# The second product of a mixture layer, computed transposed: w_out stationary and g moving

## Chip, cores and metric

The kernel runs on one core of one Trainium2 chip. The metric is the device time in microseconds (us) of one execution. Before the change the median of 3 runs is 1168.23 us (1168.09 to 1169.08).

## What is computed

The reference, cut to what matters, with 8 batches, 12 heads, 448 tokens of a batch, 64 features of a head, d_model 768 and d_ff 2048:

```python
scores = q @ k.T / sqrt(64) - log(448)          # per batch and head, 448 x 448
attn = 1 / (1 + exp(-scores))
x = (attn @ v), the heads side by side           # 3584 tokens x 768
h = x @ w_in                                     # 3584 x 2048
g = h - tanh(h)
out = g @ w_out                                  # 3584 x 768, f32
```

## The kernel before

The work goes batch by batch. The features of x lie on the partitions, so x of one batch is six tiles of 128 x 448 (features x tokens). TensorE computes with a *stationary* operand, which a weight load (LDWEIGHTS, shown as PEld) puts into the array, and a *moving* operand that streams past it; the stationary operand's columns become the partitions of the result, which lands in a PSUM bank.

To come near f32, most operands are split into a high and a low f16 half, and each product is three matmuls: high x high, high x low, low x high. The steps of one batch:

- **Attention** (`stream`, and for batch 0 `attention32`). Scores `sc` (`scores`, L393), the sigmoid `a` on ScalarE (L404), its split `ahl` on ScalarE and VectorE (L410, L411), the product with v into `acc` (`av`, L424).
- **First product** (`moe1`, `product` L772). For each of 8 pairs of 128-wide blocks of d_ff: w_in is stationary, x is moving (448 columns), result `ph`, two PSUM banks. `mix` (L804) then works off `ph`: two ScalarE activations (`u` L810, `th` L812), VectorE steps (L814, L815, L821, L825), more activations and a select (L828). `halves` (L763) writes the tile of g: its high half on ScalarE (L765), then its low half on VectorE (L766). One such tile `g` holds two blocks f of d_ff, each 128 x 448.
- **Second product** (`moe2`). In the kernel before, a 128-token slice of g is the stationary operand and a half of w_out's rows (384 of 768 columns) is the moving one. For batches 1 to 7 there are three tiles of 128 tokens; in each, the loop over the 16 blocks f runs the three products for both halves, into the banks `po0` and `po1`, and ScalarE (L889) and VectorE (L893) copy one bank each out, scaled, and SP stores it (`store`). Batch 0 takes the halves one after the other, since the second half of w_out is still being converted. The last 64 tokens are the remainder: `por` (L904) is computed with two half-wide matmuls side by side, copied by VectorE (L913) and stored in two pieces.

For batches 1 to 6, the attention of the next batch is put between the matmuls of the second product. `moe2` is a generator; after each of its steps `second` looks at `now` and issues the attention blocks whose position has come (the table `BLOCKS`, in steps of six matmuls: 8, 11, 16 and so on; `BLOCKS1` for batch 1). The rest of the last tile's `mix` and its `halves` are issued at the positions `TAIL`, 1 to 5. Batch 7 has no attention behind it. In batch 0 everything, the conversion and split of the weights too (L186, L201, L237 to L240), is laid out by hand in the string `ORDER`, one letter for a step; `P` is a step of the second product.

Each engine takes its instructions in the order of issue. `po` lies in two PSUM banks that take turns (tag `mm`), and the output tile `o` in two buffers.

Of the kernel before, what the change touches and what calls it, by code (L numbers as in the profile page):

```python
# [10 lines left out]
F32 = mybir.dt.float32  # L11
# [3 lines left out]
AF = mybir.ActivationFunctionType  # L15
ALU = mybir.AluOpType
# [3 lines left out]
P = 128  # L20
D = 64
# [12 lines left out]
class Builder:  # L34
# [5 lines left out]
    ORDER = (  # L40
        "lurmlorumsrrsrrmmlussmvvrrssvvrlrssvvrrvruvlssrurssvvrrssvlrrsvvvursrsvs"
        "vrrssvrsrrvvvvRrRrRRRMrRRRnRrRRGMRRwtMttRtRBtwRRtMwBgttMtRtRttMBttRtRttM"
        "tMBBtRttRMtBttMttMtRxtRtBRAtMtttAMtBttMttAttAttMMtAtPPtaRPRBPtBbtCaBCBAC"
        "PtFCCPBPCPPBZPPPCSBCPPBZCBCPPCCBPCCCSZBPPCCCPCXBaaAPaPPPBAPPaaaBBSPPSPSZ"
        "PSZSPPPPPPPSPBPPPZPPPNPZPSPZPSSNNPPSZPPZSSPPPPPPPPPPPP"
    )

    BLOCKS = (8, 11, 16, 20, 20, 20, 27, 32, 36, 36, 36, 43, 48, 52, 52)
# [242 lines left out]
    def w_out_scale(self, e):  # L291

        V = self.nc.vector
        self.w_out_bound(e)
        m = self.bound[e]
        total = self.sm.tile([P, 1], F32, name="wtot2")
        V.scalar_tensor_tensor(total, m, 1.05, m, op0=ALU.mult, op1=ALU.mult)
        S, inv = self.scale_of(total, f"swo{e}")
        self.Swo.append(S)
        V.tensor_copy(self.iSwo[:, e : e + 1], inv)  # L300
        h = slice(e * D, (e + 1) * D)
        V.tensor_copy(self.iSwo[h, 2:3], inv[h])

    def split_w_out(self, e):
        for f in range(0, self.NF, 2):
# [530 lines left out]
    def moe2(self, b, gs):  # L836
        nc = self.nc
        S = self.S
        ks = self.ks
        iK = self.sm.tile([P, 3], F32, name="iK")  # L840
        n = 1 if b == 0 else 3
        nc.vector.tensor_scalar(iK[:, :n], self.iSwo[:, :n], self.iSg, None, op0=ALU.mult)
        H = self.HALF
        base = b * S
        prods = ((0, 0), (0, 1), (1, 0))
        last = (self.NF - 1, 2)

        def store(o, j0, n, cols, queue=nc.sync):
            queue.dma_start(self.out[base + j0 : base + j0 + n, cols], o)

        nt = S // P

        def products(po, tk, f, e):
            for n, (x, w) in enumerate(prods):
                for i in e:
                    nc.tensor.matmul(  # L856
                        po[i][:, :H],
                        gs[f // 2][:, x, f % 2, tk * P : (tk + 1) * P],
                        self.wo[:, i * self.NF + 2 * ks[f // 2] + f % 2, w],
                        start=(f == 0 and n == 0),  # L860
                        stop=((f, n) == last),
                    )

        if b == 0:
            for e in range(2):
                for tk in range(nt):
                    po = {e: self.ps.tile([P, 512], F32, name="po", tag="mm", bufs=2)}
                    for f in range(0, self.NF, 2):
                        products(po, tk, f, (e,))
                        products(po, tk, f + 1, (e,))  # L870
                        if f + 2 == self.NF:
                            if (e, tk) == (1, 0):
                                nc.vector.tensor_scalar(iK[:, 1:], self.iSwo[:, 1:], self.iSg, None, op0=ALU.mult)
                            o = self.op.tile([P, H], F32, name="oh", tag="o", bufs=2)
                            nc.scalar.activation(o, po[e][:, :H], AF.Copy, scale=iK[:, e : e + 1])
                            store(o, tk * P, P, slice(e * H, (e + 1) * H))
                        yield 980
        else:
            for tk in range(nt):
                if b + 1 == self.B and tk % 2:  # L880
                    both = self.ps.tile([P, 2, 512], F32, name="po", tag="sc", bufs=2)
                    po = [both[:, e] for e in range(2)]
                else:
                    po = [self.ps.tile([P, 512], F32, name=f"po{e}", tag="mm", bufs=2) for e in range(2)]
                for f in range(self.NF):
                    products(po, tk, f, (0, 1))
                    if f == self.NF - 1:
                        o = self.op.tile([P, self.DM], F32, name="o", tag="o", bufs=2)
                        nc.scalar.activation(o[:, :H], po[0][:, :H], AF.Copy, scale=iK[:, 0:1])  # L889
                        if (b, tk) == (1, 0):  # L890
                            nc.scalar.activation(o[:, H:], po[1][:, :H], AF.Copy, scale=iK[:, 1:2])  # L891
                        else:
                            nc.vector.tensor_scalar(o[:, H:], po[1][:, :H], iK[:, 1:2], None, op0=ALU.mult)  # L893
                        store(o, tk * P, P, slice(0, self.DM))
                    yield 980
        nm = nt * P
        if b + 2 < self.B:
            po = self.ps.tile([P, 512], F32, name="por", tag="mm", bufs=2)
        else:
            po = self.ps.tile([P, 2, 512], F32, name="por", tag="sc", bufs=2)[:, 0]  # L900
        for f in range(self.NF):
            for n, (x, w) in enumerate(prods):
                for e in range(2):
                    nc.tensor.matmul(  # L904
                        po[e * D : (e + 1) * D, :H],
                        gs[f // 2][:, x, f % 2, nm:S],
                        self.wo[:, e * self.NF + 2 * ks[f // 2] + f % 2, w],
                        start=(f == 0 and n == 0),
                        stop=((f, n) == last),
                    )  # L910
            yield 560
        o = self.op.tile([P, H], F32, name="orem", tag="o", bufs=2)
        nc.vector.tensor_scalar(o, po[:, :H], iK[:, 2:3], None, op0=ALU.mult)  # L913
        for e in range(2):
            queue = nc.scalar if e and b + 1 == self.B else nc.sync
            store(o[e * D : (e + 1) * D], nm, S - nm, slice(e * H, (e + 1) * H), queue)


    def build(self):
        nc, tc = self.nc, self.tc  # L920

        def const(name, value, n=1):
            t = self.const.tile([P, n], F32, name=name)
            nc.vector.memset(t, value)
            return t

        self.nls = const("nls", -math.log(self.S))
        self.b1 = const("b1", B1)
        self.b2 = const("b2", B2)
        self.b3 = const("b3", -CUT * CUT)  # L930
        self.tiny = const("tiny", TINY)
        self.ih0 = const("ih0", 1.0)
        self.ihk0 = const("ihk0", KAPPA)
        self.iSwo = const("iswo", 1.0, 3)
        self.sums = [const(f"ss{i}", 0.0, 6) for i in range(2)]
        self.Swo = []
        self.sums_out, self.bound = [[], []], [None, None]
        self.xs32, self.x2b = False, []
        pieces = list(self.pieces())
        nA = 4 * self.NC  # L940
        E = mybir.EngineType
        with tc.manual_schedule(engines={E.PE, E.Activation, E.DVE, E.Pool}):
            nB = nA + self.NF + self.EARLY
            self.stage = tc.alloc_tile_pool(name="stage", bufs=2, reuse_waits="tile")
            self.blocks = self.stream()
            self.first(
                self.convert(pieces[:nA], "attention"),
                self.convert(pieces[nA:nB], "mixture"),
                self.convert(pieces[nB:], "product"),
            )  # L950
        with tc.manual_schedule(engines={E.PE, E.Activation, E.DVE, E.Pool, E.SP}):
            for b in range(1, self.B):
                self.batch(b)
        self.gp.release()
# [128 lines left out]
    def second(self, b, blocks, alone, events):  # L1083

        step = lambda: next(self.blocks)
        events += [(p, step) for p in blocks]
        scales = []

        def norms():
            scales.append(self.batch_scales(self.xs, False))  # L1090
            next(scales[0])

        if blocks:
            end = blocks[alone]
            events.append((end + 3, norms))
            events += [(p, lambda: next(scales[0], None)) for p in (end + 5, end + 7)]
        events.sort(key=lambda e: e[0])
        full = self.NF * (self.S // P)
        for k, _ in enumerate(self.moe2(b, self.gs)):
            now = k + 1 if k < full else full + (k + 1 - full) / 2  # L1100
            while events and events[0][0] <= now:
                events.pop(0)[1]()
        assert not events
# [34 lines left out]
```

## Time and profile before

| What | Value |
|---|---|
| median of 3 runs | 1168.23 us |
| lowest and highest run | 1168.09, 1169.08 us |
| span of the profiled execution (its own time, no other is given for it) | 1167.9 us |
| TensorE busy | 1155.8 us (99%) |
| VectorE (DVE) busy | 907.0 us (78%) |
| ScalarE (ACT) busy | 867.1 us (74%) |
| granted TensorE clock, mean | 1.000 |
| matmuls of the second product, full and remainder | 2304 and 768 |

The span runs from the first to the last instruction of one execution; it lies 0.3 us under the median of the runs. Rows of groups give the code line, engine, operation, output <- inputs with their shape and count, then busy time and mean duration (ns), then idle time of the engine before them and what ended it. Rows of the timeline give the start, the duration (both us, counted from the span's start), the engine, the line and the count of instructions merged. Matmuls overlap in such rows: a row's duration holds the latency of its last one, so rates are read from one row's start to the next row's start. Line numbers are those of the kernel before, unless the text says otherwise.

### The profile page before, as it was taken

The page shows a single profiled execution, that of the slowest core. Times are in us where ns is not written, and L with a number is a line of the kernel's source. Part 1 is how long each engine was busy: PE and PEld are TensorE (multiplying, and loading weights), DVE is VectorE, ACT ScalarE, POOL GpSimd, SP SyncE. Part 2 cuts the span into 40 slices and gives each one's busy share as a digit, 9 for nine tenths or more (in the row PEclk, how much of TensorE's full clock was granted, in tenths as well). Part 3 has the DMA queues.
Part 4 walks back from the last instruction along what each step waited for, and adds up shares of the span by engine and source line. Part 5 has one row for each costly group of instructions (what it writes and reads, how often), then busy time and mean ns, then how long its engine had stood idle before and what let it go on. Part 6 is the DMA issues. An engine that isn't in the chain of part 4 may idle for free.

```text
span 1167.9 us, 18941 instructions
## 1 busy us (share of the span) xinstructions
PE 1155.8 (99%) x7585; PEld 601.7 (52%) x7585; DVE 907.0 (78%) x1308; ACT 867.1 (74%) x1195; POOL 77.9 (7%) x58
## 2 busy tenths in 40 slices
PE   9999999999999999999999999999999999999998
PEld 2345434555555555555555555555555555555565
DVE  6999999789777896679867897778976799646930
ACT  7988996588975888768888588867887688745820
POOL 0000000000120002200021000200022000300000
PEclk9999999999999999999999999999999999999999
DMA  9942171000222002210022101210012100000000
GB/s 361 355 160 64 34 226 52 34 7 1 78 72 64 11 1 77 62 53 1 17 75 62 40 1 31 79 58 26 1 55 84 52 1 8 23 27 8 1 15 34
DMA packets 34056, 70.43 MB, mean 60 GB/s; under 512 B 3888, under 2 KB 21040, under 8 KB 33968
## 3 DMA queue, kind: packets, MB, share of 16 engines
q1 hardware_dynamic: 33744, 68.89, 18.2%
q8 instruction: 59, 0.97, 0.4%
q10 hardware_dynamic: 224, 0.33, 0.1%
q14 instruction: 29, 0.24, 0.1%
HBM read 58.20 MB, written 11.01 MB: 59 GB/s over the span
## 4 chain that ended last, share of the span: by engine, by line
PE 73%; ACT 1%; issue 0%; DVE 0%; ACTq 0%
PE ph L772 28%; PE po L856 27%; PE sc L393 6%; PE acc L424 6%; PE por L904 5%; ACT ahl L410 0%; ACT a L404 0%; PE pbn L343 0%; PE nm L689 0%; ACT sqn L335 0%; ACT x L438 0%; ACT Q L368 0%; DVE orem L913 0%; ACT x L453 0%; ACT o L891 0%
## 5 line engine op out<-in xcount | busy, mean ns | idle before, releaser
L856 PE MATMUL po<-wo,g 128*128 128x384 f16 x2304 | 389.2, 326 | 2.8 <-DVE wo L240 1.4
L772 PE MATMUL ph<-xhl,wi 128*128 128x448 f16 x2016 | 382.6, 352 | 0.0
L856 PEld LDWEIGHTS <-g 128*128 128x128 f16 x2304 | 220.6, 98 | 168.6 <-issue 25.3
L772 PEld LDWEIGHTS <-wi 128*128 128x128 f16 x2016 | 196.7, 98 | 185.0 <-issue 2.1
L411 DVE SCALAR_TENSOR_TENSOR ahl<-a,ahl 128x896 f16<-128x896 f32 x126 | 161.6, 1318 | 127.9 <-ACT ahl L410 127.8
L404 ACT ACTIVATE a<-sc,nls,rn 128x896 f32<-128x896 f32 x147 | 155.7, 1090 | 38.6 <-PE sc L393 38.2
L810 ACT ACTIVATE u<-ph,ih 128x896 f32<-128x896 f32 x64 | 64.4, 1006 | 77.0 <-PE ph L772 75.1
L410 ACT ACTIVATE ahl<-a 128x896 f16<-128x896 f32 x126 | 113.2, 941 | 0.6
L393 PE MATMUL sc<-Q,K 64*128 64x448 f16 x1008 | 100.8, 353 | 0.8 <-DVE th L815 0.6
L814 DVE SCALAR_TENSOR_TENSOR m<-ph,ihk,u 128x896 f32<-128x896 f32 x64 | 73.4, 1147 | 27.5 <-ACT th L812 27.2
L765 ACT ACTIVATE g<-m,Sg 128x896 f16<-128x896 f32 x64 | 66.7, 1042 | 35.2 <-DVE m L828 28.2
L828 DVE COPY_PREDICATED m<-u,th 128x896 f32<-128x896 uint32 x64 | 77.3, 1207 | 6.9 <-ACT u L827 0.9
L424 PE MATMUL acc<-ahl,vhl 128*64 128x448 f16 (+1 forms) x864 | 80.6, 356 | 0.1
L766 DVE SCALAR_TENSOR_TENSOR g<-m,Sg,g 128x896 f16<-128x896 f32 x64 | 73.4, 1146 | 6.8 <-ACT g L765 6.7
L455 POOL TENSOR_TENSOR x<-x 128x448 f32<-128x448 f32 x24 | 27.1, 1129 | 765.5 <-ACT x L438 765.5
L825 DVE SCALAR_TENSOR_TENSOR m<-q,m 128x896 f32<-128x896 f32 x64 | 69.9, 1092 | 6.7 <-DVE m L821 0.5
L982 PE MATMUL ph<-x,wi 128*128 128x448 f32 x192 | 73.8, 540 | 0.0
L815 DVE SCALAR_TENSOR_TENSOR th<-ph,ih,th 128x896 f32<-128x896 f32 x64 | 73.2, 1144 | 0.0
L821 DVE SCALAR_TENSOR_TENSOR m<-q,m 128x896 f32<-128x896 f32 x64 | 69.6, 1087 | 0.0
L827 ACT ACTIVATE u<-u,b 128x896 f32<-128x896 f32 x64 | 66.7, 1042 | 1.9
L820 ACT ACTIVATE q<-u,b 128x896 f32<-128x896 f32 x64 | 65.8, 1029 | 0.0
L824 ACT ACTIVATE q<-u,b 128x896 f32<-128x896 f32 x64 | 65.8, 1028 | 0.0
(141 smaller groups left out, 1096.1 us busy)
## 6 DMA issues: line engine op xcount, KB each, us to landing
knn<-k SPq DMA_DIRECT2D x45, 224.0 KB, 2.6
qnn<-q SPq DMA_DIRECT2D x44, 224.0 KB, 2.6
rawo<-moe_w_out SPq DMA_DIRECT2D x22, 384.0 KB, 5.1
out<-o SPq DMA_DIRECT2D x21, 384.0 KB, 2.3
raw<-moe_w_in SPq DMA_DIRECT2D x13, 512.0 KB, 8.2
vn<-v SPq DMA_DIRECT2D x24, 256.0 KB, 2.9
wo<-moe_w_in SPq DMA_DIRECT2D x11, 512.0 KB, 8.0
vn<-v SPq DMA_DIRECT2D x24, 192.0 KB, 2.4
```

What stands on the lines that cost most here:

```text
L393: self.nc.tensor.matmul(ps[i * m : (i + 1) * m, h, : self.S], K[i][r, w, c * P : c * P + m], Q[i][r, x, :], start=(n == 0), stop=(n == len ...
L404: self.nc.scalar.activation(a[:, 0], ps[:, :, : self.S], AF.Sigmoid, bias=self.nls, scale=scale)
L410: nc.scalar.activation(A[:, 0], a[:, 0], AF.Copy, scale=A_SCALE)
L411: nc.vector.scalar_tensor_tensor(A[:, 1], a[:, 0], A_SCALE, A[:, 0], op0=ALU.mult, op1=ALU.subtract)
L424: self.nc.tensor.matmul(acc[i][h * D : (h + 1) * D, : self.S], v[k, w, 2 * QT + h if half else h * QT + c], A[k, x, h], start=(n == 0 and ...
L766: nc.vector.scalar_tensor_tensor(g[:, 1], m, Sg, g[:, 0], op0=ALU.mult, op1=ALU.subtract)
L772: self.nc.tensor.matmul(ph, self.wi[:, self.slot(c, k), part, e * P : (e + 1) * P], xhl[c][:, x, :], start=(i == 0), stop=(i == len(prods) ...
L814: V.scalar_tensor_tensor(m, ps, ihk, u, op0=ALU.mult, op1=ALU.mult)
L815: V.scalar_tensor_tensor(th, ps, ih, th, op0=ALU.mult, op1=ALU.subtract)
L828: V.copy_predicated(m, u.bitcast(U32), th)
L856: nc.tensor.matmul(po[i][:, :H], gs[f // 2][:, x, f % 2, tk * P : (tk + 1) * P], self.wo[:, i * self.NF + 2 * ks[f // 2] + f % 2, w], star ...
L982: nc.tensor.matmul(ph[:, e, :S], self.fp32(self.wi, self.slot(c, k))[:, 0, e * P : (e + 1) * P], xs[c], start=(c == 0), stop=(c == self.NC ...
```

## The change

The operands of the second product change places: a 128 x 128 piece of w_out is stationary and a whole 448-token block of g is moving. The result is a tile of 128 output features x 448 tokens, six of them in a batch (index d), each summed over all 16 blocks f. The output stays transposed in memory (768 x 3584), and is transposed back on the host. The remainder of 64 tokens is gone. The tiles are copied out by ScalarE and VectorE in turn; the last tile of the last batch is copied and stored in two halves, by ScalarE with its own queue and by VectorE with SP's. A step of `moe2` is now three matmuls (six in batch 0) and `now` advances by 7/12 with each, so that `BLOCKS` keeps its numbers. `ORDER` loses 16 letters `P`.

```diff
-        "tMBBtRttRMtBttMttMtRxtRtBRAtMtttAMtBttMttAttAttMMtAtPPtaRPRBPtBbtCaBCBAC"
+        "tMBBtRttRMtBttMttMtRxtRtBRAtMtttAMtBttMttAttAttMMtAtPPtaRRBPtBbtCaBCBACP"
...
-        def products(po, tk, f, e):
+        half = self.NC // 2
+
+        def products(po, d, f):
+            e, at = d // half, d % half * P
             for n, (x, w) in enumerate(prods):
-                for i in e:
-                    nc.tensor.matmul(
-                        po[i][:, :H],
-                        gs[f // 2][:, x, f % 2, tk * P : (tk + 1) * P],
-                        self.wo[:, i * self.NF + 2 * ks[f // 2] + f % 2, w],
-                        start=(f == 0 and n == 0),
-                        stop=((f, n) == last),
-                    )
...
+                nc.tensor.matmul(
+                    po[:, :S],
+                    self.wo[:, e * self.NF + 2 * ks[f // 2] + f % 2, w, at : at + P],
+                    gs[f // 2][:, x, f % 2],
+                    start=(f == 0 and n == 0),
+                    stop=((f, n) == last),
+                )
+
+        def out(po, d):
+            iv = iK[:, d // half : d // half + 1]
+            rows = slice(d * P, (d + 1) * P)
+            o = self.op.tile([P, S], F32, name="o", tag="o", bufs=2)
+            if b + 1 == self.B and d == self.NC - 1:
+                h = S // 2
+                nc.scalar.activation(o[:, :h], po[:, :h], AF.Copy, scale=iv)
+                nc.scalar.dma_start(self.out[rows, b * S : b * S + h], o[:, :h])
+                nc.vector.tensor_scalar(o[:, h:], po[:, h:S], iv, None, op0=ALU.mult)
+                nc.sync.dma_start(self.out[rows, b * S + h : (b + 1) * S], o[:, h:])
+                return
+            if b == 0 or d % 2 or (b, d) == (1, 0):
+                nc.scalar.activation(o, po[:, :S], AF.Copy, scale=iv)
+            else:
+                nc.vector.tensor_scalar(o, po[:, :S], iv, None, op0=ALU.mult)
+            nc.sync.dma_start(self.out[rows, cols], o)
+
+        for d in range(self.NC):
+            po = self.ps.tile([P, 512], F32, name="po", tag="mm", bufs=2)
+            for f in range(self.NF):
+                products(po, d, f)
...
+                    out(po, d)
+                if b or f % 2:
+                    yield 567
...
-            now = k + 1 if k < full else full + (k + 1 - full) / 2
+            now = (k + 1) * 7 / 12
```

Three places in the order of instructions. The first is TensorE at the start of the second product of the third batch. Before, the names are `g_3893` for the batch's first tile of g and `g_4293` for its last; a weight load of g stands ahead of each matmul, and two pieces of attention (`sc`, `acc`) lie before the last tile:

```order
L772 MATMUL ph_4256<-xhl_3678,wi_96 128x448
L856 LDWEIGHTS g_3893 [waits Activation_49]
L856 MATMUL po0_4303<-wo_97,g_3893 128x384
...
L393 MATMUL sc_4365<-Q_3454,K_3448 128x448 [waits PE_49]
...
L856 LDWEIGHTS g_4183 [waits DVE_49]
...
L424 MATMUL acc_3767<-ahl_4377,vhl_3428 64x448 [waits DVE_49]
...
L856 MATMUL po1_4304<-wo_97,g_4238 128x384
L856 LDWEIGHTS g_4293
L856 MATMUL po0_4303<-wo_97,g_4293 128x384
```

Now, at the same place, `g_4040` is the last tile but one and `g_4095` the last; ahead of these rows stand 36 matmuls of the first tile `po_4105`, and the six scores are the only piece of attention before the last g:

```order
L850 MATMUL po_4105<-g_4040,wo_97 128x448 [waits Activation_49]
...
L850 MATMUL po_4105<-g_4040,wo_97 128x448 [waits DVE_49]
...
L391 MATMUL sc_4160<-Q_3320,K_3314 128x448 [waits PE_49]
...
L850 MATMUL po_4105<-g_4095,wo_97 128x448 [waits Activation_49]
...
L850 MATMUL po_4105<-g_4095,wo_97 128x448 [waits DVE_49]
...
L850 MATMUL po_4191<-g_3695,wo_97 128x448
```

The first use of the last tile of g has moved from the 85th matmul of the batch's second product to the 43rd, and it carries waits for both engines that write g.

The second place is TensorE in batch 0, around the first use of w_out's second half (`po_1752` before, `po_1832` now), with two score tiles `sc` and the third, which waits for ScalarE. Before:

```order
L343 MATMUL pbn_1732<-ss1_116,onesf_92 128x6 [waits Activation_49]
...
L856 MATMUL po_1752<-wo_97,g_641 128x384 [waits DVE_49]
...
L856 MATMUL po_1752<-wo_97,g_736 128x384 [waits DVE_49]
...
L393 MATMUL sc_1771<-Q_1561,K_1558 128x448 [waits PE_49]
...
L393 MATMUL sc_1824<-Q_1561,K_1558 128x448 [waits Activation_49]
```

Now:

```order
L341 MATMUL pbn_1709<-ss1_116,onesf_92 128x6 [waits Activation_49]
...
L850 MATMUL po_1627<-g_996,wo_97 128x448
...
L391 MATMUL sc_1741<-Q_1545,K_1542 128x448 [waits PE_49]
...
L391 MATMUL sc_1794<-Q_1545,K_1542 128x448 [waits Activation_49]
...
L850 LDWEIGHTS wo_97 [waits DVE_49]
L850 MATMUL po_1832<-g_641,wo_97 128x448
```

The first tile with the second half has moved from ahead of this attention to behind it, and two steps of the tile before (`po_1627`) lie between.

The third place is VectorE at the end of the program. Before, the copies of the last batch and the remainder's, which waits for TensorE:

```order
L766 SCALAR_TENSOR_TENSOR g<-m,Sg,g 128x896 [waits Activation_49]
L893 TENSOR_SCALAR o<-po_11679,iK 128x384 [waits DMAHW3_49,PE_49]
L893 TENSOR_SCALAR o<-po,iK 128x384 [waits DMAHW5_49,DMAHW4_49,Activation_49]
L893 TENSOR_SCALAR o<-po_11894,iK 128x384 [waits DMAHW6_49,DVE_49,PE_49]
L913 TENSOR_SCALAR orem<-por,iK 128x384 [waits DMAHW7_49,DVE_49,PE_49]
```

Now:

```order
L764 SCALAR_TENSOR_TENSOR g<-m,Sg,g 128x896 [waits Activation_49]
L872 TENSOR_SCALAR o<-po,iK 128x448 [waits DMAHW0_49,PE_49]
L872 TENSOR_SCALAR o<-po,iK 128x448 [waits DMAHW2_49,DVE_49,PE_49]
L872 TENSOR_SCALAR o<-po,iK 128x448 [waits DMAHW4_49,DVE_49,PE_49]
L866 TENSOR_SCALAR o<-po,iK 128x224 [waits DMAHW5_49,DMAHW3_49,DMAHW7_49,DMAHW1_49,Activation_49]
```

VectorE's half of the last tile (128x224) has a wait for ScalarE, whose half stands ahead of it, and none for TensorE.

More of the change, by code (lines that the diff above doesn't have):

```diff
@@ L42 @@
         "vrrssvrsrrvvvvRrRrRRRMrRRRnRrRRGMRRwtMttRtRBtwRRtMwBgttMtRtRttMBttRtRttM"
-        "tMBBtRttRMtBttMttMtRxtRtBRAtMtttAMtBttMttAttAttMMtAtPPtaRPRBPtBbtCaBCBAC"
-        "PtFCCPBPCPPBZPPPCSBCPPBZCBCPPCCBPCCCSZBPPCCCPCXBaaAPaPPPBAPPaaaBBSPPSPSZ"
-        "PSZSPPPPPPPSPBPPPZPPPNPZPSPZPSSNNPPSZPPZSSPPPPPPPPPPPP"
+        "tMBBtRttRMtBttMttMtRxtRtBRAtMtttAMtBttMttAttAttMMtAtPPtaRRBPtBbtCaBCBACP"
+        "tFCCPBPCPPBZPPCSBCPPBZCBCPPCCBPCCCSZBPCCCPCXBaaAPaPPPBAPaaaBBSPPSPSZPSZS"
+        "PPPPPPSPBPPZPPPNPZPSPZSSNNPPSZPZSSPPPP"
     )
@@ L300, in w_out_scale @@
         V.tensor_copy(self.iSwo[:, e : e + 1], inv)
-        h = slice(e * D, (e + 1) * D)
-        V.tensor_copy(self.iSwo[h, 2:3], inv[h])
     def split_w_out(self, e):
@@ L839, in moe2 @@
         ks = self.ks
-        iK = self.sm.tile([P, 3], F32, name="iK")
-        n = 1 if b == 0 else 3
+        iK = self.sm.tile([P, 2], F32, name="iK")
+        n = 1 if b == 0 else 2
         nc.vector.tensor_scalar(iK[:, :n], self.iSwo[:, :n], self.iSg, None, op0=ALU.mult)
         H = self.HALF
-        base = b * S
+        cols = slice(b * S, (b + 1) * S)
         prods = ((0, 0), (0, 1), (1, 0))
         last = (self.NF - 1, 2)
-        def store(o, j0, n, cols, queue=nc.sync):
-            queue.dma_start(self.out[base + j0 : base + j0 + n, cols], o)
@@ L851, in moe2 @@
-        nt = S // P
-        def products(po, tk, f, e):
+        half = self.NC // 2
+        def products(po, d, f):
+            e, at = d // half, d % half * P
             for n, (x, w) in enumerate(prods):
-                for i in e:
-                    nc.tensor.matmul(
-                        po[i][:, :H],
-                        gs[f // 2][:, x, f % 2, tk * P : (tk + 1) * P],
-                        self.wo[:, i * self.NF + 2 * ks[f // 2] + f % 2, w],
-                        start=(f == 0 and n == 0),
-                        stop=((f, n) == last),
-                    )
@@ L864, in moe2 @@
[L864 to L916, printed above, removed]
+                nc.tensor.matmul(
[5 more added lines that the diff above has]
+                )
@@ L919, in build @@
+        for d in range(self.NC):
+            po = self.ps.tile([P, 512], F32, name="po", tag="mm", bufs=2)
+            for f in range(self.NF):
+                products(po, d, f)
+                if f == self.NF - 1:
+                    if (b, d) == (0, half):
+                        nc.vector.tensor_scalar(iK[:, 1:], self.iSwo[:, 1:], self.iSg, None, op0=ALU.mult)
+                    out(po, d)
+                if b or f % 2:
+                    yield 567
     def build(self):
@@ L933, in build @@
         self.ihk0 = const("ihk0", KAPPA)
-        self.iSwo = const("iswo", 1.0, 3)
+        self.iSwo = const("iswo", 1.0, 2)
         self.sums = [const(f"ss{i}", 0.0, 6) for i in range(2)]
@@ L1097, in second @@
         events.sort(key=lambda e: e[0])
-        full = self.NF * (self.S // P)
         for k, _ in enumerate(self.moe2(b, self.gs)):
-            now = k + 1 if k < full else full + (k + 1 - full) / 2
+            now = (k + 1) * 7 / 12
             while events and events[0][0] <= now:
@@ L1131 @@
     }
-    shape = (B * S, H * D)
+    shape = (H * D, B * S)
     args["out"] = nc.dram_tensor("out", shape, F32, kind="ExternalOutput").ap()
@@ L1136 @@
     r = run_bass_kernel_spmd(nc, [arrays], core_ids=[0])
-    return r.results[0]["out"]
+    return np.ascontiguousarray(r.results[0]["out"].T)
```

## Prediction

> **What bounds the kernel now.** I read the page's head first, then TensorE's waits, the groups of matmuls by shape, and the timeline where the second product starts and ends.
>
> ```profile
> span 1167.9 us, 18941 instructions
> ...
> PE 1155.8 (99%) x7585; PEld 601.7 (52%) x7585; DVE 907.0 (78%) x1308; ACT 867.1 (74%) x1195; POOL 77.9 (7%) x58
> ```
>
> TensorE (PE) is busy for 1155.8 of 1167.9 us. Of its waits, the one that is longest in total (us, times, longest):
>
> ```profile
> PE po L856 <- DVE wo L240: 1.4, 3, 0.6
> ```
>
> None comes to more than these 1.4 us. So there are two ways to move the end: change what TensorE's instructions take, or make it wait where it did not. A wait on TensorE cannot be made good later, since there is no idle time to take it from. The second product's matmuls, and those of the first product, whose moving operand already has the new width of 448:
>
> ```profile
> L856 PE MATMUL po<-wo,g 128*128 128x384 f16 x2304 | 389.2, 326 | 2.8 <-DVE wo L240 1.4 <-DVE g L766 0.7 <-ACT g L765 0.3
> L772 PE MATMUL ph<-xhl,wi 128*128 128x448 f16 x2016 | 382.6, 352 | 0.0
> ...
> L904 PE MATMUL por<-wo,g 128*64 128x384 f16 x768 | 64.9, 327 | 0.0
> ```
>
> **Term 1, the matmuls.** Per batch 288 full matmuls of 384 columns and 96 half-wide ones of the remainder become 288 full ones of 448: 110592 + 48 pairs x 384 = 129024 columns before, 288 x 448 = 129024 now. What is left is the cost per instruction. The last batch, where no attention lies between, and the remainder of the first batch:
>
> ```profile
> 1079.82 29.30 PE L772 MATMUL ph<-xhl,wi 128*128 128x448 f16 x154
> 1108.95 46.96 PE L856 MATMUL po<-wo,g 128*128 128x384 f16 x288
> 1155.84 7.99 PE L904 MATMUL por<-wo,g 128*64 128x384 f16 x96
> ...
> 219.50 7.99 PE L904 MATMUL por<-wo,g 128*64 128x384 f16 x96
> 227.43 2.82 PE L772 MATMUL ph<-xhl,wi 128*128 128x448 f16 x14
> ```
>
> From start to start, 448 columns take (1108.95 - 1079.82)/154 = 189.2 ns, 384 take (1155.84 - 1108.95)/288 = 162.8 ns, and the remainder 227.43 - 219.50 = 7.93 us with the switch out of its half-wide form. Before: 46.89 + 7.93 = 54.82 us a batch. Now: 288 x 0.1892 = 54.48. The gain is 0.34 us a batch, 2.7 in eight. With w_out stationary instead of g a weight load could cost otherwise; the first product loads w_in in just this form behind just such matmuls, so I take its 189.2; one ns off would be 2.3 us in all, either way.
>
> [...]
>
> **Term 2, the last g.** A tile of the output sums over all of g. Before, a tile of tokens took both halves of w_out at each step f, so the last tile of g (f = 14 and 15) was touched after 14 x 6 = 84 matmuls. Now a tile of 128 features takes three matmuls per f and touches it after 42. When does TensorE get there, and when is the last g ready? In the third batch, TensorE, then ScalarE, then VectorE:
>
> ```profile
> 426.92 7.96 PE L856 MATMUL po<-wo,g 128*128 128x384 f16 x48
> 434.81 0.74 PE L393 MATMUL sc<-Q,K 64*128 64x448 f16 x6
> 435.49 3.10 PE L856 MATMUL po<-wo,g 128*128 128x384 f16 x18
> ```
>
> ```profile
> 435.99 1.04 ACT L765 ACTIVATE g<-m,Sg 128x896 f16<-128x896 f32 x1 [2.95 <-DVE m L828]
> ```
>
> ```profile
> 429.06 1.15 DVE L814 SCALAR_TENSOR_TENSOR m<-ph,ihk,u 128x896 f32<-128x896 f32 x1
> ...
> 431.31 1.15 DVE L766 SCALAR_TENSOR_TENSOR g<-m,Sg,g 128x896 f16<-128x896 f32 x1
> ...
> 434.77 1.19 DVE L828 COPY_PREDICATED m<-u,th 128x896 f32<-128x896 uint32 x1
> 437.07 1.15 DVE L766 SCALAR_TENSOR_TENSOR g<-m,Sg,g 128x896 f16<-128x896 f32 x1 [1.11 <-ACT g L765]
> ```
>
> The first product ends at 426.92, and only then do ScalarE and VectorE work off its last tile, in a chain of their own: the high half of the last g is written at 437.03, the low half at 438.22, 11.3 us after the second product began. Nothing in that chain hangs on the second product, and the order of ScalarE and VectorE in it is unchanged. So its times stay, and TensorE's arrival moves. Before, the 84th matmul lay behind two pieces of attention as well, past 438.22, and nothing waited. Now, by the new order, 42 matmuls end at 426.92 + 42 x 0.1892 = 434.87, six scores follow as before (0.08 for the switch, 0.68 to 435.49), and the first matmul with the last g is due at 435.63. The high half is there at 437.03 + 0.04 (the handover between the two g rows). Two matmuls use it; the third, due at 436.01, needs the low half at 438.26. Lost: 2.25 us. The order of batches 2 to 6 is the same there: 5 x 2.25 = 11.25. The tile before causes nothing: its low half is ready at 432.46, and due after 36 matmuls, at 433.73. In the last batch no scores lie between:
>
> ```profile
> 1118.02 1.04 ACT L765 ACTIVATE g<-m,Sg 128x896 f16<-128x896 f32 x1 [2.94 <-DVE m L828]
> ...
> 1119.10 1.15 DVE L766 SCALAR_TENSOR_TENSOR g<-m,Sg,g 128x896 f16<-128x896 f32 x1 [1.11 <-ACT g L765]
> ```
>
> Due for the third matmul: 1108.95 + 44 x 0.1892 = 1117.27; ready: 1120.25 + 0.04. Lost: 3.0 us. In the second batch the 42 matmuls have the score and value products of two blocks behind them first:
>
> ```profile
> 293.96 2.58 PE L424 MATMUL acc<-ahl,vhl 128*64 128x448 f16 x30
> 296.48 3.10 PE L856 MATMUL po<-wo,g 128*128 128x384 f16 x18
> ```
>
> ```profile
> 294.03 1.15 DVE L766 SCALAR_TENSOR_TENSOR g<-m,Sg,g 128x896 f16<-128x896 f32 x1
> ```
>
> TensorE comes back to the product at 296.48, the last g is ready at 295.18: nothing lost. Sum of term 2: 14.3 us.
>
> **Term 3, the first batch.** There the splits of w_out and the attention set the pace, and some waits go:
>
> ```profile
> 192.11 0.74 PE L393 MATMUL sc<-Q,K 64*128 64x448 f16 x6 [0.21 <-ACT a L404]
> 192.79 5.50 PE L856 MATMUL po<-wo,g 128*128 128x384 f16 x31
> 198.87 6.82 PE L856 MATMUL po<-wo,g 128*128 128x384 f16 x41 [0.57 <-DVE wo L240]
> ```
>
> At 192.11 TensorE waits for ScalarE, whose work hangs on VectorE's splits. I take this as a gate: what is won or lost ahead of it is levelled there. Behind it, before: 132 matmuls, 21.49 us, a loss of 198.87 - 192.79 - 31 x 0.1628 = 1.03 (the second half of w_out came late), and 7.93 for the remainder, 30.45 in all. Now 156 x 0.1892 = 29.51, and the second half's first tile starts two steps later, so I count that wait as gone. Gain 0.94, of which 0.34 is in term 1: 0.6 more. If the gate opens earlier it is up to 1.5 more, if a new wait comes, 1 less.
>
> **Term 4, the end and the rest.** The last tile is copied out in halves by ScalarE and VectorE, but in the order VectorE's half waits for ScalarE's.
>
> ```profile
> 1155.84 0.58 ACT L889 ACTIVATE o<-po,iK 128x384 f32<-128x384 f32 x1 [14.91 <-PE po L856]
> ...
> 1163.88 0.62 DVE L913 TENSOR_SCALAR orem<-por,iK 128x384 f32<-128x384 f32 x1 [7.31 <-PE por L904]
> ```
>
> 384 columns take 0.58 and 0.62 us; 224 I put between 0.35 and 0.5 each, one after the other about 0.95, against 0.62: 0.3 later, between 0 and 0.5. The other copies, 6 of 448 instead of 7 of 384 columns, lie beside TensorE on engines with a fifth of their time free: nothing. A PSUM bank comes round after a whole other tile (9.1 us), so no wait there. Stores on SP's queue are more and smaller; the loads behind them are issued a block ahead: nothing.
>
> **Sum** against the profiled span: 1167.9 - 2.7 + 14.3 - 0.6 + 0.3 = 1179.2. The median of the runs shown, 1168.23, lies 0.3 above the span: 1179.5.
>
> **Rivals.** (a) The last g is not late: not slower but faster. ScalarE and VectorE would have to finish it 2.25 us sooner in each batch; then only terms 1, 3 and 4 are left, 1179.5 - 14.3 = 1165.2. Against it: from 429.06 VectorE goes from one step of the chain to the next, and the change takes none of it away. 5 in 100.
>
> (b) The waits cool TensorE's clock. The kernel's first matmuls show a slow phase:
>
> ```profile
> 1.19 3.59 PE L97 MATMUL warm<-onesb 128*128 128x512 bf16 x8 [1.19 <-DVE nls L924]
> ...
> 6.42 1.90 PE L97 MATMUL warm<-onesb 128*128 128x512 bf16 x8
> ```
>
> The same eight matmuls take 3.59 us, then 1.90. If each of the six waits brings such a phase back, it costs 1.7 each: 1179.5 + 10.2 = 1189.7. No wait in this trace is as long as the new ones, so it is open. 6 in 100. [...]
>
> (c) Something in ScalarE's or VectorE's order shifts and halves the loss: 1172.3. 4 in 100.
>
> (d) A matmul costs the same whatever its width, so that fewer of them win: 2304 of 448 columns at 162.8 ns instead of 189.2 are 60.8 us less, 1118.7. The two rates above, on neighbouring matmuls, speak against it: 1 in 100. [...]
>
> **How the numbers follow.** My forecast has 84 in 100, with 1176 to 1183 from the bounds: 1 ns per matmul, 0.3 us per wait, 1.5 in the first batch. The range 1175 to 1184 leaves out (a) to (d), 16 in 100. Slower by over 0.2% (2.3 us, about what a measurement of this kernel can tell): 0.92, with (b) and half of (c); faster: 0.06, from (a) and (d); within: 0.02.
>
> **What would show it.** In the new profile the second product's matmuls stand 189 ns apart; TensorE waits for ScalarE's and then VectorE's g in six batches, some 2 us each with a longer one at the end, and not in the second batch; the wait for w_out is gone. I am wrong if these waits are absent, if matmuls after them run slow, or if the product's matmuls are not at 189 ns.

## The result and the profile after

The changed kernel takes 1182.86 us (median of 4 runs, 1182.01 to 1185.94), the kernel before 1168.16 in the same comparison (4 runs, 1167.81 to 1169.08). The ratio is 1.0127, interval 1.0115 to 1.014: slower by 14.7 us. The forecast was 1179.5.

The page's head for the profiled execution, whose own time is 1182.27 us:

```profile
span 1180.3 us, 17408 instructions
...
PE 1156.3 (98%) x6816; PEld 561.5 (48%) x6817; DVE 902.4 (76%) x1299; ACT 868.3 (74%) x1195; POOL 77.7 (7%) x58
```

TensorE is busy for as long as before (1156.3 us against 1155.8), but the span is 12.4 us longer. So nearly all of the lost time shows as idle time on TensorE. The longest of its waits (us in total, times, longest):

```profile
PE po L850 <- ACT g L763: 9.0, 6, 2.0
PE po L850 <- DVE g L764: 3.9, 6, 0.6
PE po L850 <- ACT o L870: 3.1, 1, 3.1
```

The first two lines are the forecast waits: six times for the high half of the last g, six times for its low half. The third is a wait that was not forecast.

TensorE's timeline (start, duration, line, operation, count; in brackets the wait ahead and what ended it) where the second product of the third batch starts, and then the same place in the fourth batch:

```profile
424.61 8.11 PE L850 MATMUL po<-g,wo 128*128 128x448 f16 x42
432.65 0.74 PE L391 MATMUL sc<-Q,K 64*128 64x448 f16 x6
434.79 0.54 PE L850 MATMUL po<-g,wo 128*128 128x448 f16 x2 [1.40 <-ACT g L763]
435.97 4.30 PE L850 MATMUL po<-g,wo 128*128 128x448 f16 x13 [0.65 <-DVE g L764]
440.20 1.31 PE L391 MATMUL sc<-Q,K 64*128 64x448 f16 x12
```

```profile
565.88 8.11 PE L850 MATMUL po<-g,wo 128*128 128x448 f16 x42
...
576.05 0.54 PE L850 MATMUL po<-g,wo 128*128 128x448 f16 x2 [1.38 <-ACT g L763]
577.24 2.62 PE L850 MATMUL po<-g,wo 128*128 128x448 f16 x13 [0.65 <-DVE g L764]
579.79 1.31 PE L391 MATMUL sc<-Q,K 64*128 64x448 f16 x12
```

The pattern is the forecast one: 42 matmuls, six scores, a wait, two matmuls, a wait. In the fourth batch the third matmul with the last g was due at 565.88 + 44 x 0.1892 + 0.76 for the scores = 574.97 and started at 577.24, a loss of 2.27 us. The two blocks differ in the row behind the waits. The same 13 matmuls take 577.24 to 579.79, 2.55 us, in the fourth batch, and 435.97 to 440.20, 4.23 us, in the third: there TensorE's granted clock was 0.50 from 435.99 to 439.40, as the windows further down show, and 1.00 at the same place in the fourth.

In the last batch no scores lie between:

```profile
1119.00 8.11 PE L850 MATMUL po<-g,wo 128*128 128x448 f16 x42
1129.12 0.54 PE L850 MATMUL po<-g,wo 128*128 128x448 f16 x2 [2.02 <-ACT g L763]
1130.31 46.32 PE L850 MATMUL po<-g,wo 128*128 128x448 f16 x244 [0.65 <-DVE g L764]
```

Due at 1119.00 + 44 x 0.1892 = 1127.32, started at 1130.31: 2.99 us lost.

The times from one second product's start to the next, read from the two timelines, show where the 12.4 us of span lie:

| Stretch | before | after | difference |
|---|---|---|---|
| start of the run to the first second product | 130.68 | 129.01 | -1.67 |
| first batch | 151.24 | 151.60 | +0.36 |
| second | 145.00 | 144.00 | -1.00 |
| third | 137.79 | 141.27 | +3.48 |
| fourth to sixth, each | 137.79 | 139.59 | +1.80 |
| seventh | 130.87 | 134.34 | +3.47 |
| last second product to the end of the span | 58.95 | 61.30 | +2.35 |

I take the first row for a difference between two executions and not for the change, whose lines all run later. The trace before has two waits of TensorE there, 0.75 us at 26.51 and 1.16 at 69.71, which the trace after does not have; in the trace of a kernel with the old operands (below), with the same code up to there, the first is absent, the second takes 0.26, and the first second product starts at 130.02. That is most of why the medians lie further apart (14.7 us) than the two spans.

### The profile page after: what moved, and what is told of

The parts are those of the page before. It is cut to its first block, busy times and chain, and to the rows that moved or that the text cites. A ratio compares the mean times of both kernels' runs of the same rounds, so it can differ in the third digit from the quotient of the medians.

```text
span 1180.3 us, 17408 instructions
## 1 busy us (share of the span) xinstructions
PE 1156.3 (98%) x6816; PEld 561.5 (48%) x6817; DVE 902.4 (76%) x1299; ACT 868.3 (74%) x1195; POOL 77.7 (7%) x58
## 4 chain that ended last, share of the span: by engine, by line
PE 90%; DVE 5%; ACT 3%; issue 1%; DMA 0%; DVEq 0%; ACTq 0%
PE po L850 32%; PE ph L770 32%; PE acc L422 9%; PE sc L391 9%; PE ph L950 6%; DVE g L764 1%; DVE m L826 1%; DVE m L812 1%; ACT u L808 1%; DVE m L823 1%; ACT g L763 1%; DVE m L819 1%; PE cs L207 1%; PE warm L97 1%; ACT th L810 1%
## 5 line engine op out<-in xcount | busy, mean ns | idle before, releaser
L850 PE MATMUL po<-g,wo 128*128 128x448 f16 x2304 | 455.3, 354 | 16.0 <-ACT g L763 9.0
L850 PEld LDWEIGHTS <-wo 128*128 128x128 f16 x2304 | 221.1, 98 | 243.1 <-issue 48.3
```

Source lines behind the costliest of these rows:

```text
L850: nc.tensor.matmul(po[:, :S], self.wo[:, e * self.NF + 2 * ks[f // 2] + f % 2, w, at : at + P], gs[f // 2][:, x, f % 2], start=(f == 0 and ...
```

## Experiments

My theory was that the loss is the early use of the last g, which comes from the order of the loops and not from the exchange of the operands. The rivals: the exchanged operands are themselves dearer, or slowed-down matmuls account for much of the loss. Open as well was the unforecast wait in the first batch, which could be harmless if the attention behind it is a gate that levels it.

### Two tiles held back together

Both first tiles of features run up to f = 13, and only then take the last g. In this and the other reordering kernels the loop then runs over `steps`.

```diff
+        steps = [(d, f) for d in range(self.NC) for f in range(self.NF)]
+        if b:
+            cut = self.NF - 2
+            ends = [(d, f) for d in range(2) for f in range(cut, self.NF)]
+            steps[: 2 * self.NF] = [(d, f) for d in range(2) for f in range(cut)] + ends
```

> The changed kernel with another order of the same matmuls in batches 1 to 7: the first two feature tiles run blocks f = 0 to 13 one after the other, and only then f = 14 and 15 of each, so that the last tile of g is first needed after 84 matmuls (15.9 us) instead of 42 (7.9 us). Late-g theory: all six waits for g go, and with them the stretches at half clock; left are the gains of 2.7 and 1.0 us against the kernel before and 0.3 us at the end, so about 1168.2 - 3.4 = 1164.8 us, clock 1.000. Rival, the swap itself costs (w_out as the stationary operand, 448 columns, the six copies): the time stays at 1178 us or more. A new wait of up to 0.7 us a batch for the first tile's PSUM bank would give 1169.

Measured: 1183.73 us (1182.78 to 1183.79) against 1168.54, ratio 1.013, interval 1.0115 to 1.0145. Nothing was gained. Every wait for g is gone, and TensorE's longest wait is another:

```profile
PE po L850 <- ACT o L870: 18.0, 7, 3.4
```

TensorE's timeline at the end of the two tiles of the third batch, then ScalarE's at the same place:

```profile
450.85 2.44 PE L850 MATMUL po<-g,wo 128*128 128x448 f16 x12
455.72 1.86 PE L850 MATMUL po<-g,wo 128*128 128x448 f16 x9 [2.42 <-ACT o L870]
```

```profile
453.37 1.78 ACT L408 ACTIVATE ahl<-a 128x896 f16<-128x896 f32 x2
455.05 0.62 ACT L870 ACTIVATE o<-po,iK 128x448 f32<-128x448 f32 x1
```

The two tiles end six matmuls apart (the row of 12 holds both ends), so neither of the two PSUM banks has been copied out when the next tile is due. Both copies stand behind the attention's splits in their engines' orders: ScalarE's starts at 455.05, VectorE's, behind 2.09 us of splits, at 456.35, and TensorE goes on at 455.72, as soon as ScalarE's is done. The batch takes 139.92 us from start to start, no better than the 139.59 of the changed kernel. I had priced this wait too low. The experiment shows that the waits for g can be taken away, but not yet what they cost.

### The old operands in the new order of loops

The kernel before, with g still stationary, but with one half of w_out after the other in all batches, so that a tile takes three matmuls per f as in the changed kernel (copies of the second half go to VectorE from the third batch on).

```diff
-        if b == 0:
+        if True:
             for e in range(2):
                 for tk in range(nt):
...
-                            nc.scalar.activation(o, po[e][:, :H], AF.Copy, scale=iK[:, e : e + 1])
+                            if b < 2 or e == 0:
+                                nc.scalar.activation(o, po[e][:, :H], AF.Copy, scale=iK[:, e : e + 1])
+                            else:
+                                nc.vector.tensor_scalar(o, po[e][:, :H], iK[:, e : e + 1], None, op0=ALU.mult)
```

> The kernel before with only the loop order changed in batches 1 to 7: one half of w_out after the other, as batch 0 has it, so that the last tile of g is needed after 42 matmuls of 384 columns (6.84 us). No operand is swapped, the remainder stays. Late-g theory: the third matmul with the last g is due at 434.84 us in the third batch and has its operand at 438.26, 3.4 us lost in each of batches 2 to 6 and 4.2 in the last, 21.3 in all: 1189.5 us, up to 1199.7 if each wait brings a stretch of half clock of 1.7 us. Rival, the swap costs: about 1168 us.

Measured: 1207.04 us (1206.04 to 1208.94) against 1168.54, ratio 1.0329, interval 1.0311 to 1.0346. Its longest wait, and TensorE in the third batch:

```profile
PE po L856 <- ACT g L765: 21.4, 8, 3.2
```

```profile
431.79 6.99 PE L856 MATMUL po<-wo,g 128*128 128x384 f16 x42
441.92 0.50 PE L856 MATMUL po<-wo,g 128*128 128x384 f16 x2 [3.14 <-ACT g L765]
443.11 0.94 PE L856 MATMUL po<-wo,g 128*128 128x384 f16 x4 [0.69 <-DVE g L766]
443.98 1.30 PE L393 MATMUL sc<-Q,K 64*128 64x448 f16 x6
```

The same wait, with the operands as they were: the order of the loops brings it. It is longer than in the changed kernel because the 42 matmuls are narrower and the scores come only behind the wait; the second batch waits too. The loss is larger than expected for three reasons: the expectation had put the scores (0.76 us) ahead of the wait, the second batch takes 150.55 us instead of 145.00, and the clock fell to 0.50 in all seven batches that wait (at 444 us six scores take 1.23 us from start to start instead of 0.68).

### The waits filled with other matmuls

Ahead of the first use of the last g TensorE gets six matmuls (nine in the last batch) whose result nothing uses. They lie in the time in which it would wait.

```diff
+                if b > 1 and (d, f) == (0, self.NF - 2):
+                    fill = self.ps.tile([P, 2, 512], F32, name="fill", tag="sc", bufs=2)[:, 0]
+                    moving = self.onesb[:, None, :].to_broadcast([P, 4, P])
+                    for _ in range(9 if b + 1 == self.B else 6):
+                        nc.tensor.matmul(fill, self.onesb, moving, start=True, stop=True)
```

> The changed kernel with idle matmuls ahead of the first use of the last g (6 of 512 columns at 216 ns, 1.3 us, in batches 2 to 6, 9 in the last, 1.9 us); their result is used by nothing. They fill the wait for g's high half without making it longer, and leave that for the low half (0.65 us). Theory that an idle TensorE loses its clock: no stretch at half clock, mean clock 1.000, about 1182.9 - 3.4 = 1179.5 us with runs within 1 us of one another. Rival, the slow stretches come from something else (a load on the whole core, or chance): two to four of them as before, 1182 to 1186 us.

Measured: 1180.7 us (1180.6 to 1181.03) against 1168.54, ratio 1.0106, interval 1.0091 to 1.0122. TensorE in the third batch:

```profile
434.20 0.74 PE L391 MATMUL sc<-Q,K 64*128 64x448 f16 x6
434.88 1.47 PE L882 MATMUL fill<-onesb 128*128 128x512 bf16 x6
436.34 0.54 PE L850 MATMUL po<-g,wo 128*128 128x448 f16 x2
437.52 2.62 PE L850 MATMUL po<-g,wo 128*128 128x448 f16 x13 [0.65 <-DVE g L764]
440.08 1.31 PE L391 MATMUL sc<-Q,K 64*128 64x448 f16 x12
```

The third matmul starts as late as before (due at 426.16 + 44 x 0.1892 + 0.76 = 435.24, started at 437.52), but the 13 behind it take 2.56 us. Batches three to six now take 139.60 us each, and none 141.27. The granted clock is 1.00 behind all six waits, and TensorE is busy for 0.81 of the windows that hold them. So I put the slowed matmuls of the changed kernel down to TensorE's idleness; they cost 141.27 - 139.59 = 1.68 us a time, and the loss of 2.25 us a batch is the waiting itself. The runs lie within 0.4 us of each other, those of the changed kernel within 3.9; of those the slowest, 1185.94 us, has a mean clock of 0.994 and the other three 0.997, which by an estimate, 0.003 of 1183 us at 1.7 us a stretch, would be about two stretches more.

One stretch at half clock (0.50) is left, where none was expected, from 178.96 to 182.37. It lies in the first batch, whose wait for a PSUM bank was not filled:

```profile
178.54 2.03 PE L850 MATMUL po<-g,wo 128*128 128x448 f16 x6 [3.35 <-ACT o L870]
```

That batch takes 153.14 us (282.17 - 129.03) instead of 151.60, which is more than the 1.2 us between 1180.7 and the expected 1179.5.

### The last g later still

Three activations whose result nothing uses stand on ScalarE ahead of the last g, from the third batch on.

```diff
+            if b > 1:
+                late = self.tp.tile([P, 2, self.S], F32, name="late", tag="t")
+                for _ in range(3):
+                    self.nc.scalar.activation(late, self.late[0][0], AF.Copy)
             self.finish_g()
```

> The changed kernel with the last tile of g made later by three activations of 1.03 us on ScalarE (3.1 us) in batches 2 to 7; their result is used by nothing. The waits for g grow from 2.2 to 5.3 us, those for the high half from 1.4 and 2.0 to 4.5 and 5.1. Late-g theory: 18.6 us more for the waits. Theory that the clock falls when TensorE idles through a window of some 3.4 us: all six waits now bring a stretch at half clock (10.2 us instead of 3.4), 1182.9 + 18.6 + 6.8 = 1208.3 us. If the stretches come by chance in a third of the waits: 1201.5 us. If TensorE had slack to make up for a late g: less than 1190 us.

Measured: 1206.02 us (1205.55 to 1206.95) against 1168.54, ratio 1.0324, interval 1.0308 to 1.0339. Its longest wait, and windows of one core (from:to, length, then busy time and count of PE, PEld, DVE, ACT, POOL; granted clock, DMA share, GB/s) around the wait of the third batch:

```profile
PE po L850 <- ACT g L763: 25.8, 6, 4.8
```

```profile
435.12:438.53 3.41, 0.00 (x0) 0.00 (x0) 0.00 (x0) 3.33 (x4) 0.00 (x0) 1.00 0.00 0
438.53:441.94 3.41, 2.63 (x7) 0.95 (x7) 2.89 (x4) 3.38 (x6) 0.00 (x0) 0.50 0.00 0
441.94:445.36 3.42, 3.42 (x11) 1.16 (x11) 1.50 (x3) 0.68 (x4) 0.00 (x0) 0.50 0.28 79
```

Now all six waits have a stretch at a granted clock of 0.50 behind them, not two. The third to sixth batch take 144.86, 144.17, 143.78 and 143.56 us. The third matmul with the last g of the third batch starts 440.21 - 435.14 = 5.07 us late (due 426.06 + 44 x 0.1892 + 0.76), against 435.97 - 433.69 = 2.28 in the changed kernel (due 424.61 + 44 x 0.1892 + 0.76). These 2.79 us more are what ScalarE is late with: it starts the last g at 437.95, 2.81 us behind the start of the added activations at 435.14. Of the 7.52 us over an undisturbed batch (137.34, below), 5.07 are waiting, and the other 2.45 I put down to the clock.

### The first tile held open

The remedy without the clash of copies: the first tile's last two steps (f = 14 and 15) come after eight steps of the second tile, in all batches but the first.

```diff
+        steps = [(d, f) for d in range(self.NC) for f in range(self.NF)]
+        if b:
+            n = self.NF
+            steps[n - 2 : n + 8] = steps[n : n + 8] + steps[n - 2 : n]
```

> The changed kernel with another order of the same matmuls in batches 1 to 7: the first feature tile stops after f = 13, f = 0 to 7 of the second follow, then f = 14 and 15 of the first, then the rest of the second. The last tile of g is first needed after 66 matmuls (12.5 us, against 11.4 when it is ready in the last batch, which has no attention between), and the first tile is complete 24 matmuls (4.5 us) before the third needs its PSUM bank, with its copy ahead of the next attention block on its engine. Theory: the waits for g were the loss, and two_tiles_first only put a wait for a PSUM bank in their place, since there the copies came 12 matmuls before the bank was needed and behind an attention block. Then no wait of either kind is left in batches 1 to 7, no stretch at half clock there, and 1168.5 - 2.7 - 1.0 - 0.3 = 1164.5 us is measured. Rival, the swap of the operands itself costs: 1178 us or more, with no waits to show for it. Between them, 1170, if the copies still come late.

Measured: 1166.68 us (12 runs, 1164.95 to 1168.41) against 1168.37 (17 runs, 1167.24 to 1170.83), ratio 0.9985, interval 0.9976 to 0.9993. Moving this one use takes 16.2 us off the changed kernel's 1182.86. Of the long waits only the first batch's is left, and TensorE behind it:

```profile
PE po L850 <- ACT o L870: 3.0, 1, 3.0
```

```profile
178.80 1.63 PE L850 MATMUL po<-g,wo 128*128 128x448 f16 x6 [3.04 <-ACT o L870]
...
180.68 2.52 PE L391 MATMUL sc<-Q,K 64*128 64x448 f16 x18
...
193.62 0.74 PE L391 MATMUL sc<-Q,K 64*128 64x448 f16 x6
```

Batches three to six take 137.34 us, all the same. So the waits for g cost 139.59 - 137.34 = 2.25 us a batch, and the exchange itself gains 137.79 - 137.34 = 0.45. What is missing to the expected time lies in the first batch: 153.59 us instead of 151.60, since here the clock fell behind its wait (0.50 from 179.62 to 183.03; 18 scores take 2.46 us to the next start, in the changed kernel 1.36). The two of the 12 runs with a mean clock of 1.000 took 1164.95 and 1165.99 us.

### The first tile held open, and one step of the first batch later

In the first batch one step of the second product (`P`) moves behind the last column sum of w_out (`C`) and an attention block, so that ScalarE has time for the copy that frees the bank.

```diff
-        "tFCCPBPCPPBZPPCSBCPPBZCBCPPCCBPCCCSZBPCCCPCXBaaAPaPPPBAPaaaBBSPPSPSZPSZS"
+        "tFCCPBPCPPBZPPCSBCPPBZCBCPPCCBPCCCSZBPCCCCXBPaaAPaPPPBAPaaaBBSPPSPSZPSZS"
```

> As first_tile_held_open, and one letter of the hand-written order of batch 0 moved: the first step of the third feature tile comes behind the attention block that follows it, so that it doesn't stand waiting for its PSUM bank (3.1 us in the changed kernel's profile, ScalarE's copy being late). Gate theory: what is won ahead of the scores that wait for ScalarE (at 192.11 us before the change) is lost again there, so the time is that of first_tile_held_open within 0.5 us though the wait of 3.1 us is gone. Rival, that wait is on the path: 3 us faster.

Measured: 1163.56 us (5 runs, 1163.18 to 1164.43) against 1168.37, ratio 0.9959, interval 0.9947 to 0.9971: faster than the kernel before by 4.8 us, and than the changed one by 19. TensorE in the first batch:

```profile
176.27 0.33 PE L201 MATMUL wl<-stb,onesb 128*128 128x384 bf16 x1 [0.52 <-DVE stb L181]
...
178.78 5.83 PE L850 MATMUL po<-g,wo 128*128 128x448 f16 x30 [0.81 <-ACT o L870]
...
190.38 0.74 PE L391 MATMUL sc<-Q,K 64*128 64x448 f16 x6
```

The wait has shrunk from 3.04 to 0.81 us, with a new one of 0.52 ahead of it, and the first batch from 153.59 to 150.27: 3.3 us, 1.7 of waiting, and about as much for the stretch at half clock that is gone. The time went down by as much (1166.68 to 1163.56); it lies 1.4 and 2.4 us under the two runs of the experiment before that kept full clock. The scores that were to be the gate start at 190.38 instead of 193.62 and wait for nothing, so what was lost ahead of them was not levelled there. Whether they would level a gain stays open: ScalarE is done with what they need at 190.30 (189.22 + 1.08), 0.08 us before they start.

## Why the prediction was right, and where not

| Step | forecast | measured |
|---|---|---|
| Term 1, per batch | -0.34 | -0.45 |
| Term 2, per batch, third to seventh | +2.25 | +2.25 |
| Term 2, last batch | +3.0 | +2.99 |
| Term 2, second batch | 0 | 0 |
| Term 3, first batch with its share of term 1 | -0.94 | +0.36 |
| Term 4, the end | +0.3 | about -0.4 |
| clock behind the waits (rival b: 10.2) | 0 | +3.4 |

**Term 2 was right in place and size.** The last g is finished at the same distance as before from the first product's end, and TensorE's arrival moved: 5 x 2.25 + 2.99 = 14.2 us. The reordering that moves only this first use takes the loss away, and the old operands in the new loop order have it too; so rival (a) and the exchange of operands as a cause are ruled out.

**Term 1** was right in its rate. The groups of the two products with 448 columns (busy time, then the mean of one in ns):

```profile
L850 PE MATMUL po<-g,wo 128*128 128x448 f16 x2304 | 455.3, 354 | 16.0 <-ACT g L763 9.0 <-DVE g L764 3.9 <-ACT o L870 3.1
L770 PE MATMUL ph<-xhl,wi 128*128 128x448 f16 x2016 | 382.5, 352 | 0.0
```

With w_out stationary a matmul takes what it takes with w_in: 354 and 352 ns, latency included. From start to start, 42 of them and the switch to the scores take 432.65 - 424.61 = 8.04 us; 42 x 0.1892 + 0.08 are 8.03. That rules out rival (d). The 0.11 us a batch beyond the forecast was not followed up.

**The failed step: the waits were taken to cost no clock.** That was my estimate; no trace had shown it. Rival (b) came true in two of six waits. Windows of the changed kernel, columns as above:

```profile
176.58:179.99 3.41, 1.43 (x9) 0.62 (x10) 2.72 (x4) 1.93 (x6) 1.32 (x1) 1.00 0.17 65
432.58:435.99 3.41, 1.36 (x10) 0.51 (x10) 2.30 (x3) 2.26 (x3) 0.00 (x0) 1.00 0.00 0
435.99:439.40 3.41, 3.41 (x10) 1.37 (x10) 3.17 (x5) 2.39 (x6) 0.00 (x0) 0.50 0.00 0
572.52:575.93 3.41, 2.15 (x14) 0.88 (x13) 2.29 (x2) 0.97 (x2) 0.00 (x0) 1.00 0.00 0
...
992.36:995.77 3.41, 1.62 (x11) 0.50 (x9) 2.20 (x3) 2.01 (x2) 0.00 (x0) 1.00 0.00 0
995.78:999.19 3.41, 3.15 (x9) 1.28 (x9) 3.37 (x6) 2.63 (x7) 0.00 (x0) 0.50 0.00 0
1125.48:1128.89 3.41, 1.62 (x9) 0.73 (x8) 2.30 (x3) 0.86 (x1) 0.00 (x0) 1.00 0.00 0
```

The clock is at half for 3.41 us, from 435.99 and from 995.78, each time behind a window of that length in which TensorE was busy for 1.36 and 1.62 of 3.41 us. The two falls are 559.79 us apart, 164 times 3.4133, and all the windows above lie on the grid of that step. The fourth batch's wait is as long (1.38 and 0.65 us, in the third 1.40 and 0.65), but lies across a boundary of this grid: the window up to 575.93 has 2.15 us of work in it, and the clock stays at 1.00. So waits of one length cost 1.68 us of clock in the third batch and none in the fourth, and I put that down to where they lie against the grid. That separates these two, but it does not settle every case: the last batch's window from 1125.48 has as much work in it as the one from 992.36, and the first batch's from 176.58 less, and nothing fell behind these two. The forecast had the size of a stretch right (1.7) and its chance too low; 1179.5 + 3.4 would have been 1182.9.

**Term 3 failed in its gate.** ScalarE's copies of the first and second tile of features, and TensorE's wait for the second's bank:

```profile
151.81 0.62 ACT L870 ACTIVATE o<-po,iK 128x448 f32<-128x448 f32 x1
...
177.90 0.61 ACT L870 ACTIVATE o<-po,iK 128x448 f32<-128x448 f32 x1
```

```profile
174.81 0.67 PE L201 MATMUL wl<-stb,onesb 128*128 128x384 bf16 x3
178.56 1.29 PE L850 MATMUL po<-g,wo 128*128 128x448 f16 x6 [3.08 <-ACT o L870]
```

The second tile was complete at 174.97, its copy came late behind ScalarE's other work, and TensorE lost 3.1 us. "What is won or lost ahead of it is levelled there" was wrong for a loss, as the last experiment shows: the scores stand 62.79 us behind the start of the batch's second product (191.80 - 129.01), before 61.43 (192.11 - 130.68). Behind the scores the term was right: 88.81 us to the next second product (280.61 - 191.80) instead of 89.81, a gain of 1.00 against 0.94, with the waits for w_out gone. The two together are the +0.36.

The prediction's "A PSUM bank comes round after a whole other tile (9.1 us), so no wait there" held for batches two to eight and failed in this one. The first tile had been copied out at 152.43, but the third did not get its bank: in this batch the column sums of w_out (`wl`, the row ahead of the wait) take their bank from the same two (L200, tag `mm`) and held it from 155.96 on. So the third tile had to follow in the bank of the second.

**Term 4** had the mechanism right and the sum wrong. The end, on ScalarE and VectorE:

```profile
1176.71 0.45 ACT L864 ACTIVATE o<-po,iK 128x224 f32<-128x224 f32 x1 [17.52 <-PE po L850]
...
1177.19 0.45 DVE L866 TENSOR_SCALAR o<-po,iK 128x224 f32<-128x224 f32 x1 [8.93 <-ACT o L864]
```

VectorE's half waits for ScalarE's, 0.9 us in all as estimated. But each half's store lands 1.7 us after its issue, those of the remainder took 2.2 and 2.4; I had not counted the stores. The last store lands 2.75 us behind TensorE's end instead of 3.08. From TensorE's end to the end of the span it is 1167.9 - 1163.83 = 4.07 us before and 1180.3 - 1176.63 = 3.67 after, hence the -0.4; but of the five experiments that end in the same way as the changed kernel three have about 4.0 there, so how much of it the change gives is open.

**From span to time.** I set the time 0.3 us above the span. The profiled execution after lies 1182.27 - 1180.3 = 2.0 above, and every run here that gives both lies 1.7 to 2.2 above, the kernel before 1.7 to 1.9. The span of before, 1167.9, was thus probably that of an execution slower than the median by some 1.5 us, which goes with the first row of the stretches above (-1.67). The forecast adds its terms to the median as well as to the span, so it was not hurt.

Together: 14.2 (term 2) + 3.4 (clock) - 3.5 (second to last batch otherwise) + 0.36 (first batch) - 0.4 (end) = 14.1 us, against 14.7 between the medians; the profiled execution, 1182.27, lies 0.6 below the median of its kernel. Apart from the clock, the misses nearly cancelled, and that was luck: the first batch came out 1.3 us worse than forecast, the later ones 1.1 better (3.5 instead of 7 x 0.34) and the end 0.7 better. In the second batch 0.55 of the gain of 1.00 is beyond term 1. Two short waits of the kernel before, 0.14 us each at 293.96 and 310.32, are gone there; the rest was not traced.

## What to carry to other kernels

When the order of loops over an accumulation changes, ask how many instructions now lie ahead of the first use of the operand that is made last, and compare its finish with that arrival in the trace; here the exchange was worth 1.7 us of gain or 14.7 us of loss depending on where two steps of one tile stood, and 4.8 us of gain with one step of the first batch moved as well. TensorE was busy for 98% of the span here, and waits that held it up by 2.27 us made a batch 2.25 us longer (139.59 against 137.34). Before moving tiles apart or together, look whether the copy that frees their bank stands behind other work in its engine's order, and what else takes its bank from the same few.

## What the runs showed of the hardware

- From 100 us on, six traces show TensorE's granted clock at 0.50 for a time: the changed kernel's and those of all experiments but the last. These stretches were 3.41 or 6.83 us long. In the kernel with the old operands four of them began at 443.69, 587.05, 730.41 and 873.77 us, 143.36 apart, 42 times 3.4133.
- With each of these traces laid out in windows of 3.413 us that start where its stretches start, every window in which TensorE was busy for a share of at most 0.40 was followed by one at half clock. One with 0.47 was too, three others with 0.42 to 0.47 were not, and above that none that ran at full clock was. The first batch's wait for a bank shows both sides: the window that holds most of it was busy for 0.42 in the changed kernel, and the clock stayed; for 0.12, 0.20 and 0.24 in the kernels with the waits filled, the last g later still and the first tile held open, and it fell. A stretch ended behind a window at half clock that was busy for 0.83 or more, and went on behind those with 0.33, 0.73 and 0.77.
- In the changed kernel two of six waits that two matmuls (0.54 us) broke had such a stretch behind them. With matmuls that nothing uses put into the waits, six of them or 1.47 us in the third batch, none of the six had, and nothing was delayed: the third matmul with the last g of that batch came 2.28 us late with them (437.52 - 435.24) and without (435.97 - 433.69).
- A half-clock stretch of 3.41 us cost 1.68 us where TensorE had work throughout: 13 matmuls took 4.23 us in place of 2.55.
